# Expert 0's rows gathered before the last token tile is written, the last tile's rows added on TensorE, two weight steps put off, and 20 places of small matmuls moved

## The chip, the cores and the metric

One core of one Trainium2 chip runs the whole program. The metric is the device time of one execution in microseconds (us), the median of several. TensorE (PE) multiplies matrices into PSUM, VectorE (DVE) and ScalarE (ACT) read PSUM and do elementwise work, GpSimd (POOL) does elementwise work and issues the indirect DMAs, SyncE (SP) issues the plain DMAs. Each engine works through its own instructions in order.

## What is computed

```
def _attn_ref(q, k, v):                       # B, H, S, D = 4, 8, 768, 64
    for t in range(S):
        state = gamma * state + outer(k[:, :, t], v[:, :, t])
        y[:, :, t] = scale * q[:, :, t] @ state

def _moe_ref(x, w_in, w_out):                 # 3072 x 512, 512 x 2048, 2048 x 512
    h = x @ w_in
    sp = np.where(h > 20.0, h, np.log1p(np.exp(np.minimum(h, 20.0))))
    return (h * np.tanh(sp)) @ w_out

def _moe2_ref(x, w_gate, w1, w2):             # 8 experts of 384 tokens each
    logits = x @ w_gate
    # all (token, expert) pairs in falling order of logit; a token goes to the first
    # expert that still has room (cap = N // E = 384)
    for e in range(E):
        mask = assigned == e
        out[mask] = np.maximum(x[mask] @ w1[e], 0.0) @ w2[e]
```

## The kernel before

Attention and the first feed-forward layer run over 8 groups of 384 tokens (`NG`, `G`), each of three tiles of 128 (`CPG`, `C`). `h_phase(g)` computes the hidden layer of a group into one of two buffers `G` (GB[0], GB[1]), `logits(g)` the gate's logits from it, and `x_phase(g)` the layer's output: 48 matmuls of 512 columns per tile into a PSUM bank "px", which ACT and DVE split into two half-precision parts (`xr`, with the row's scale in its last two places) and SP writes to the table `x_rows` in DRAM (L622). Every product is made of such high and low parts, three matmuls for one (`mm3`, L525, the line of nearly all matmuls).

Then come the experts. Expert r takes its 384 rows out of `x_rows` by three indirect DMAs (L890, issued on POOL) with the list of its tokens, `IDX[r]`. They are turned so that the model dimension lies on the partitions (`xt`): for expert 0 by 24 transposes on TensorE (L902) and three copies (L903), for the others by a DMA transpose (L354). `expert(r)` runs 96 matmuls of 384 columns (first half, weights W1) and 72 of 512 (second half, weights W2), with its weights in WIN (even r) or WOUT (odd r).

Beside this run three side programs. `route_round(r)` finds by five digits (0, 2, 4, 6, 8 in the names below) which tokens round r gives to which expert: for each digit a comparison on DVE (L686), 24 small matmuls `pc`, a small DVE step (L731), one matmul `pn`, and DVE again (L736, L740); at its end two matmuls `pp`. `route_list(r)` makes `IDX[r]` from it (L686 into `amt`, then 24 matmuls `pl`, L819). `weights(i)` loads the expert's weights W1 (i = 0) or W2 (i = 1) by an indirect DMA of 2 MB (L862) into one half of RAW, sums their squares on ACT (L868), totals them with one matmul `pt`, and splits them into two parts in four pieces (ACT L228 and DVE L229).

The order on TensorE is written out by the program: a `Weave` runs a main generator (the large matmuls) and after each piece of it the side programs that are due; a side program yields (wait, cost) in the planner's microseconds, most of them from the table `KN`. `KN['rs'][r]` holds the offsets of the 12 waits of round r, `KN['fs'][r]` those of the weight steps. ACT is in program order too from the last group on; the order on DVE and POOL is chosen by a scheduler. In the tail, `x_phase(7)` (3 tiles) is followed by the one tile of group 5 that was put off (`late`), then by `tokens()`, which gathers, and by `expert(0)`:

```
    wv.run(x_phase(NG - 1))
    wv.run(x_phase(NG - 3, late, GB[0]))
    XD.append(1)
    wv.add(tokens())
```

Of the kernel before, what the change touches and what calls it, by code (L numbers as in the profile page):

```python
# [1213 lines left out]
```

## Time and profile before

| | |
|---|---|
| median of 3 runs | 1097.4 us (1096.71 to 1100.52) |
| profiled execution | 1102.12 us, of which the span from the first to the last instruction is 1100.2 us |
| granted clock of TensorE, mean | 0.947 of full speed |
| busy in the span | PE 965.7, DVE 766.8, ACT 664.3, POOL 404.3 us |

Busy time is the time in which an engine had an instruction at work; matmuls are pipelined, so neighbouring ones overlap. Idle time of an engine that nobody waits for costs nothing.

### The profile page before, as it was taken

The numbers are of one execution on the slowest core, as the hardware profiler recorded it, in microseconds if no ns is written. First come the engines' busy times: TensorE is split into PE (matmuls) and PEld (weight loads), VectorE is DVE, ScalarE is ACT, GpSimd is POOL, SyncE is SP. The second block draws the span as 40 slices with busy tenths as digits, with TensorE's granted clock in tenths as the row PEclk, the third lists the DMA queues.
The fourth block names the chain that finished last, engine by engine and source line by source line (L and its number), as shares of the span: only waits on it lengthen the run. The fifth ranks groups of instructions, "written<-read, shape, count | busy, mean of one in ns | idle before, by whom it ended". The sixth has DMA issues, their size and how long they took to land.

```text
span 1100.2 us, 19751 instructions
## 1 busy us (share of the span) xinstructions
PE 965.7 (88%) x7897; PEld 558.3 (51%) x7897; DVE 766.8 (70%) x1742; ACT 664.3 (60%) x1010; POOL 404.3 (37%) x289
## 2 busy tenths in 40 slices
...
PEclk9959988878999999999999999999699999999999
...
GB/s 316 173 156 42 106 192 38 39 91 167 27 53 86 41 49 87 39 64 62 49 87 83 45 39 1 10 117 114 159 177 164 179 148 153 233 84 263 140 29 29
DMA packets 108812, 113.65 MB, mean 103 GB/s; under 512 B 92464, under 2 KB 92592, under 8 KB 106672
## 3 DMA queue, kind: packets, MB, share of 16 engines
q1 hardware_dynamic: 102576, 66.24, 23.5%
...
## 4 chain that ended last, share of the span: by engine, by line
PE 46%; DVE 23%; issue 12%; ACT 5%; DMA 4%; POOL 4%; SPq 0%; another core or an unknown queue 0%; POOLq 0%; ACTq 0%; DVEq 0%
PE ph L525 18%; PE px L525 18%; DVE ld L686 2%; DVE WIN L229 2%; DVE WOUT L229 2%; DMA yh<-WOUT 1%; DVE RAW L571 1%; DVE ld L373 1%; PE py L434 1%; POOL out_dram L937 1%; DVE G L574 1%; DVE RAW L555 1%; DMA ld<-in_qkv_dram 1%; DVE G L920 1%; DMA G<-x_rows,GQ 1%
## 5 line engine op out<-in xcount | busy, mean ns | idle before, releaser
L525 PE MATMUL ph<-xt,WIN 128*128 128x384 f16 x1728 | 330.8, 334 | 14.2 <-DVE RAW L555 6.3
L525 PE MATMUL px<-WOUT,G 128*128 128x512 f16 x1248 | 312.9, 386 | 2.1 <-DVE WOUT L229 1.5
L525 PEld LDWEIGHTS <-WIN 128*128 128x128 f16 x1920 | 187.4, 101 | 155.6 <-issue 31.7
L525 PEld LDWEIGHTS <-G 128*128 128x128 f16 x1728 | 165.7, 99 | 185.9 <-issue 18.6
L577 POOL TENSOR_TENSOR G<-RAW,G 128x1536 f16<-128x1536 f32 (+1 forms) x32 | 102.0, 3186 | 98.1 <-DVE G L574 78.5
L555 DVE TENSOR_SCALAR RAW<-ph 128x384 f32<-128x384 f32 x124 | 68.2, 551 | 44.2 <-PE ph L525 43.7
L406 POOL TENSOR_TENSOR amt<-amt 128x512 f16<-128x512 f32 x40 | 53.6, 1341 | 122.7 <-DVE amt L403 85.9
L562 ACT ACTIVATE RAW<-RAW,zt,ch 128x1536 f32<-128x1536 f32 x32 | 53.3, 1666 | 43.8 <-DVE RAW L555 40.3
L325 ACT ACTIVATE junk<-ld 128x512 bf16<-128x512 f32 x63 | 39.6, 628 | 62.5 <-DMA ld<-in_qkv_dram 61.4
L868 ACT ACTIVATE junk<-RAW 128x1024 bf16<-128x1024 f32 x64 | 67.5, 1055 | 6.2 <-DMA RAW<-in_w1p_dram,MASK 5.5
L571 DVE TENSOR_TENSOR RAW<-RAW 128x1536 f32<-128x1536 f32 (+1 forms) x33 | 56.5, 1712 | 13.8 <-ACT RAW L570 13.7
L223 POOL TENSOR_TENSOR RAW<-ld,RAW 128x512 f16<-128x512 f32 x34 | 46.5, 1384 | 43.5 <-ACT RAW L222 41.8
L862 POOL DMA_INDIRECT RAW<-in_w1p_dram,MASK x8 | 8.0, 1000 | 144.0 <-ACT G L919 45.9
L228 ACT ACTIVATE WOUT<-RAW,se 128x1024 f16<-128x1024 f32 x32 | 36.0, 1148 | 35.3 <-DVE se L195 35.3
L920 DVE TENSOR_TENSOR G<-G,G 128x384 f16<-128x384 f32 x64 | 35.5, 554 | 31.3 <-ACT G L919 31.1
L400 DVE TENSOR_TENSOR amt<-pa,MASK 128x512 f32<-128x512 f32 x38 | 26.1, 687 | 37.7 <-PE pa L399 30.4
L525 PEld LDWEIGHTS <-WOUT 128*128 128x128 f16 x384 | 36.9, 99 | 24.1 <-issue 0.7
L937 POOL DMA_INDIRECT out_dram<-G,MASK x18 | 25.7, 1426 | 62.5 <-ACT G L936 57.3
L570 ACT ACTIVATE RAW<-RAW 128x1536 f32<-128x1536 f32 (+1 forms) x33 | 47.7, 1445 | 0.4
L563 ACT ACTIVATE RAW<-RAW 128x1536 f32<-128x1536 f32 x32 | 47.2, 1476 | 0.4
L525 PE MATMUL px<-WIN,G 128*128 128x512 f16 x192 | 45.3, 388 | 1.3 <-DVE G L920 0.8
L223 POOL TENSOR_TENSOR STH<-SC,STH 64x256 f16<-64x256 f32 x34 | 29.6, 871 | 45.1 <-ACT STH L222 42.2
...
## 6 DMA issues: line engine op xcount, KB each, us to landing
...
ld<-in_qkv_dram SPq DMA_DIRECT2D x3, 256.0 KB
```

What stands on the lines that cost most here:

```text
L223: (V if pool in ("V", "E") else P).tensor_tensor(lo, src, hi, op=OP.subtract)
L229: V.scalar_tensor_tensor(lo, src, s, hi, op0=OP.mult, op1=OP.subtract)
L406: (P if mode[1] == "P" else V).tensor_tensor(amh[:, j, 1], am, amh[:, j, 0], op=OP.subtract)
L525: T.matmul(p, a, b, start=i == 0, stop=i == n - 1)
L555: V.tensor_scalar(hs[:, f], p[:, :G], 1.0 / 65536.0, None, op0=OP.mult)
L562: A.activation(th, hs, AF.Tanh, scale=ch[:, q:q + 1], bias=z)
L563: A.activation(th, th, AF.Arctan, scale=-0.5, bias=0.5)
L570: A.activation(th[:, w], th[:, w], AF.Sin, scale=-2.0, bias=math.pi / 2)
L571: (V if hm[1] == 'V' else P).tensor_tensor(th[:, w], th[:, w], hs[:, w], op=OP.mult)
L577: (P if lo == 'P' else V).tensor_tensor(gb[:, 1, o], th[:, w], gb[:, 0, o], op=OP.subtract)
L868: A.activation(junk(1024), RAW[:, o:o + 1024], AF.Square, accum_out=ss[:, j:j + 1])
L920: V.tensor_tensor(hid[:, 1, f], hs, hid[:, 0, f], op=OP.subtract)
```

## The change

The tail is put into another order. First a tile of zeros is written over the last 128 rows of `x_rows`. Then come tiles 0 and 1 of group 7, the tile of group 5, and, as soon as the first list is there, the three gathers for expert 0 (`first_rows`), which find zeros in the place of the last tile's rows. The last tile of group 7 is computed after their issue. `first_x` then turns the gathered rows by multiplying them with the identity (24 matmuls of 128 columns, into PSUM as f32) and adds to each bank the last tile's rows straight from `xr` in SBUF, by 24 matmuls with a 0/1 matrix that says which of its rows belongs into which column (`FIRST["cols"]`, made on DVE in `route_list(0)`). Six copies, three on ACT and three on DVE, bring the sums to `xt`; before, 24 transposes and three copies on DVE did it. The rows are gathered a second time, after the last tile has been written, only for the scales in their last two places, into the buffers of expert 1's rows, from where three DVE copies in `prep_x(1)` save them.

Two weight steps are put off: the loads of expert 1's weights wait in the program until the first gathers are issued, and the four pieces of expert 0's W2 are split after `first_x`. In the table, 20 of the 96 entries of `rs` change (rounds 1 to 7; one of round 1, two of round 2, the rest of rounds 3 to 7) and one of `fs`; one round's line shows what such a change looks like.

```diff
-rs=[..., [1.46, -2.35, 0.04, -0.29, 0.13, -2.18, 0.42, -0.4, 0.45, 0.03, 1.16, -4.07], ...
+rs=[..., [-1.04, -2.35, 0.04, -0.29, 0.13, -0.18, -1.58, -0.4, 0.45, 0.03, 3.56, -5.57], ...
-fs=[..., [0.0, -1.5, -0.61, 0.29]]
+fs=[..., [0.0, -1.5, 2.89, 0.29]], ..., g0=[0.5, 2.2, 1.5]
@@ -620,9 +620,11 @@
                 V.tensor_scalar(xr[:, 2 * DM:].bitcast(F32), i_t, cx, None, op0=OP.mult)
             r = g * G + c * C
             SY.dma_start(xbuf[r:r + C, :], xr)
+            XR[0] = xr
             yield PC[0] * 0.216
 
 
+    XR, FIRST = [None], {}
     RT, IDX, EWI, EWF = {}, {}, {}, []
 
     def route_setup():
@@ -813,6 +815,14 @@
         V.tensor_scalar(pjv, pjf[:, 0, :, None].to_broadcast([128, NT, VR]), 1.0, None, op0=OP.add)
         for t in range(0, NT, 8):
             against(oh[:, t:t + 8], pjv, OP.is_equal, len(DIGITS) - 1, slice(t, t + 8))
+        if r == 0:
+
+            e3 = rt("e3", [CPG], BF)
+            for jt in range(CPG):
+                V.tensor_scalar(e3[:, jt:jt + 1], pjf[:, 1, NT - 1:], float(jt), None, op0=OP.is_equal)
+            FIRST["cols"] = rt("cols", [CPG, C], F16)
+            V.tensor_tensor(FIRST["cols"], oh[:, NT - 1, None, :].to_broadcast([128, CPG, C]),
+                            e3[:, :, None].to_broadcast([128, CPG, C]), op=OP.mult)
         yield max(0.0, KN['lw'] + KN['rs'][r][11]), 0.0
         pl = ps.tile([128, CPG, 2], F32, name=f"pl{r}x11x", tag="pm")
         for t in range(NT):
@@ -847,7 +857,7 @@
     def weights(i):
         src = (w1p, w2p)[i]
         for r in range(E):
-            while r not in EWI or (r == 1 and KN['ga'][i] and 0 not in XTE):
+            while r not in EWI or (r == 1 and ((KN['ga'][i] and 0 not in XTE) or "rows" not in FIRST)):
                 yield 0.5, 0.0
             W = EWB[r % 2]
             ei = EWI[r]
@@ -869,7 +879,8 @@
                 yield KN['qs'], 0.0
             yield max(0.0, KN['tw'] + KN['fs'][r][2 + i]), 0.2
             SW[i, r] = pow2(total(ss, 4, "tote", f"pt{r}x{2 + i}x"), f"se{i}", 3)
-            while (r > 1 and r - 2 not in (H2, OUT)[i]) or (r == 1 and not XD):
+
+            while (r > 1 and r - 2 not in (H2, OUT)[i]) or (r == 1 and not XD) or (r == 0 and i and 0 not in XTE):
                 yield 0.5, 0.0
             for j in range(4):
                 o = i * 4096 + j * 1024
@@ -882,26 +893,61 @@
                 V.tensor_scalar(ie, SW[0, r][1], SW[1, r][1], 65536.0, op0=OP.mult, op1=OP.mult)
                 SC[r] = ie
 
+    def first_rows():
+
+        for c in range(CPG):
+            P.indirect_dma_start(out=XG[c], out_offset=None, in_=xbuf,
+                                 in_offset=bass.IndirectOffsetOnAxis(ap=IDX[0][:, c:c + 1], axis=0))
+        FIRST["rows"] = True
+
+    def first_x():
+
+        xt = wk.tile([128, 2, KD, G], F16, name="xt", tag="xt", bufs=2)
+        XTE_[0] = xt
+        pp = {}
+
+        def part(c, a, w, cols, first):
+            if first:
+                pp[c, a] = ps_any().rearrange("p (k t) -> p k t", k=KD)
+            for k in range(KD):
+                o = (a * KD + k) * 128
+                T.matmul(pp[c, a][:, k], w[:, o:o + 128], cols, start=first and k == 0, stop=not first and k == KD - 1)
+            if not first:
+                o = xt[:, a, :, c * C:(c + 1) * C]
+                with tc.high_priority():
+                    if a:
+                        V.tensor_copy(o, pp[c, a])
+                    else:
+                        A.activation(o, pp[c, a], AF.Copy)
+
+        yield KN['g0'][0], 0.0
+        for c in range(2):
+            for a in range(2):
+                part(c, a, XG[c], identh, True)
+        yield KN['g0'][1], 1.0
+        for c in range(CPG):
+            for a in range(2):
+                if c == 2:
+                    part(c, a, XG[c], identh, True)
+                part(c, a, XR[0], FIRST["cols"][:, c, :], False)
+
+        for c in range(CPG):
+            P.indirect_dma_start(out=XG[CPG + c], out_offset=None, in_=xbuf,
+                                 in_offset=bass.IndirectOffsetOnAxis(ap=IDX[0][:, c:c + 1], axis=0))
+        yield KN['g0'][2], 1.7
+
     def prep_x(r):
         xt = wk.tile([128, 2, KD, G], F16, name="xt", tag="xt", bufs=2)
         XTE_[r] = xt
+        if r == 1:
+            FIRST["scale"] = rt("fs", [CPG])
+            for c in range(CPG):
+                V.tensor_copy(FIRST["scale"][:, c:c + 1], XG[CPG + c][:, 2 * DM:2 * DM + 2].bitcast(F32))
         for c in range(CPG):
             xg = XG[(r % 2) * CPG + c]
             P.indirect_dma_start(out=xg, out_offset=None, in_=xbuf,
                                  in_offset=bass.IndirectOffsetOnAxis(ap=IDX[r][:, c:c + 1], axis=0))
-            if r:
-                turned(xt, c, xg[:, :2 * DM])
-        if r == 0:
-
-            yield 10.0, 0.0
-            for c in range(CPG):
-                p = ps_any().bitcast(F16).rearrange("p (a k t) -> p a k t", a=2, k=KD)
-                for a in range(2):
-                    for k in range(KD):
-                        o = (a * KD + k) * 128
-                        T.transpose(p[:, a, k], XG[c][:, o:o + 128], identh)
-                V.tensor_copy(xt[:, :, :, c * C:(c + 1) * C], p)
-            return
+            turned(xt, c, xg[:, :2 * DM])
         yield KN['gx'], 0.0
 
     def expert(r):
@@ -921,10 +967,13 @@
             yield PC[0] * 0.163
         while r not in SC:
             yield 0.5
+        while r == 0 and "scale" not in FIRST:
+            yield 0.5
         fac = rt("fac", [CPG], bufs=3)
         for c in range(CPG):
             xg = XG[(r % 2) * CPG + c]
-            V.tensor_scalar(fac[:, c:c + 1], xg[:, 2 * DM:2 * DM + 2].bitcast(F32), SC[r], None, op0=OP.mult)
+            xs = xg[:, 2 * DM:2 * DM + 2].bitcast(F32) if r else FIRST["scale"][:, c:c + 1]
+            V.tensor_scalar(fac[:, c:c + 1], xs, SC[r], None, op0=OP.mult)
         H2.add(r)
         for c in range(CPG):
             p = ps_any()
@@ -1073,8 +1122,11 @@
         for r in range(E):
             while r not in IDX or (r > 0 and r - 1 not in RUN) or (r > 1 and r - 2 not in H2):
                 yield 1.0, 0.0
-            yield KN['tk'], 0.0
-            yield from prep_x(r)
+            if r:
+                yield KN['tk'], 0.0
+                yield from prep_x(r)
+            else:
+                yield from first_x()
             XTE[r] = XTE_[r]
 
     wv = Weave(tc)
@@ -1147,8 +1199,14 @@
     wv.run(x_phase(NG - 2))
     for c in late:
         SY.dma_start(GB[0][:, :, :, c * C:(c + 1) * C], gbuf[c])
-    wv.run(x_phase(NG - 1))
+    zr = wk.tile([128, ROW], F16, name="xr", tag="xr", bufs=2)
+    V.memset(zr, 0.0)
+    SY.dma_start(xbuf[N - C:, :], zr)
+    wv.run(x_phase(NG - 1, range(CPG - 1)))
     wv.run(x_phase(NG - 3, late, GB[0]))
+    need(lambda: 0 in IDX)
+    first_rows()
+    wv.run(x_phase(NG - 1, range(CPG - 1, CPG)))
     XD.append(1)
     wv.add(tokens())
     for r in range(E):
```

On POOL, from the first weight load of the experts on (`in_w1p_dram` and `in_w2p_dram` are W1 and W2, `x_rows` the gathers, `out_dram` the scatters of finished rows), before:

```order
172 L862 DMA RAW<-in_w1p_dram,MASK 128x4096
173 L862 DMA RAW<-in_w2p_dram,MASK 128x4096
174 L862 DMA RAW<-in_w1p_dram,MASK 128x4096
175 L890 DMA G_67<-x_rows,MASK 128x1026 x6
176 L862 DMA RAW<-in_w2p_dram,GQ 128x4096
177 L862 DMA RAW<-in_w1p_dram,MASK 128x4096
178 L937 DMA out_dram<-G_67,MASK 3072x512
```

and in the changed kernel:

```order
172 L872 DMA RAW<-in_w1p_dram,MASK 128x4096
173 L872 DMA RAW<-in_w2p_dram,MASK 128x4096
174 L872 DMA RAW<-in_w1p_dram,MASK 128x4096
175 L899 DMA G_67<-x_rows,MASK 128x1026 x3
176 L935 DMA G_67<-x_rows,MASK 128x1026 x3
177 L948 DMA G_67<-x_rows,MASK 128x1026 x3
178 L872 DMA RAW<-in_w2p_dram,GQ 128x4096
179 L872 DMA RAW<-in_w1p_dram,MASK 128x4096
```

The first gathers (L899) still stand behind expert 1's W1 load, the third load; between them and expert 1's gathers (L948) stand the second gathers for the scales (L935).

On TensorE, between the last large matmul of the last tile and expert 0's first (`identh` is the identity, `xt` expert 0's turned rows), before:

```order
11431 L729 MATMUL pc2x2x<-MASK,ld 128x8
11432 L734 LDWEIGHTS onesb
11433 L734 MATMUL pn2x3x<-MASK,onesb 128x8
11434 L185 MATMUL pt1x2x<-sse_8619,onesf 128x4
11435 L902 LDWEIGHTS G_67
11436 L902 MATMUL ph<-identh,G_67 128x128
...
11483 L525 LDWEIGHTS WIN
11484 L525 MATMUL px<-xt,WIN 128x384
```

and in the changed kernel (`STH` holds the 0/1 matrix):

```order
11285 L525 MATMUL px<-WOUT,G_68 128x512
11286 L914 LDWEIGHTS G_67
11287 L914 MATMUL ph<-identh,G_67 128x128
...
11318 L731 LDWEIGHTS ld
11319 L731 MATMUL pc2x0x<-MASK,ld 128x8
...
11366 L829 LDWEIGHTS amt
11367 L829 MATMUL pl1x11x<-GQ,amt 128x6
...
11414 L914 LDWEIGHTS xr
11415 L914 MATMUL ph<-STH,xr 128x128
```

Of round 2, before had `pc` and `pn` of digits 0 and 2 ahead of the transposes; now the first digit's `pc` and list 1's `pl` stand between the 16 identity matmuls of the first two row tiles and the matmuls with the 0/1 matrix, and `pc2x2x` comes only inside expert 0.

On DVE, from the end of round 1 to the last tile's eviction (`WIN` is expert 0's weights, `xr` the tile), before:

```order
1024 L779 COPY MASK<-pp1x10x 128x48
1025 L229 SCALAR_TENSOR_TENSOR xr<-px,st,xr 128x512
1026 L781 SCALAR_TENSOR_TENSOR MASK<-MASK 128x48
1027 L229 SCALAR_TENSOR_TENSOR WIN<-RAW,se_8544,WIN 128x1024
1028 L783 TENSOR_TENSOR GQ<-MASK 128x48
1029 L229 SCALAR_TENSOR_TENSOR WIN<-RAW,se_8544,WIN 128x1024
1030 L784 TENSOR_TENSOR GQ<-GQ,pp1x10x 128x48
1031 L229 SCALAR_TENSOR_TENSOR WIN<-RAW,se_8544,WIN 128x1024
```

and in the changed kernel, a little later in the same stretch:

```order
1061 L688 TENSOR_TENSOR ld<-MASK,ld 128x3072
1062 L192 TENSOR_SCALAR sta<-sst 128x1
1063 L688 TENSOR_TENSOR amt<-GQ,ld 128x1024
1064 L195 TENSOR_SCALAR st<-sta 128x1
1065 L196 TENSOR_SCALAR st<-sta 128x1
1066 L688 TENSOR_TENSOR amt<-GQ,ld 128x1024
1067 L620 TENSOR_SCALAR xr<-st,cx 128x1
1068 L229 SCALAR_TENSOR_TENSOR xr<-px,st,xr 128x512
1069 L688 TENSOR_TENSOR amt<-GQ,ld 128x1024
```

The four pieces of W2 (three of them shown) are gone from this stretch and stand inside expert 0; the last tile's `xr` now follows the comparison of round 2's first digit and two of list 1's three.

## Rows read from the trace of the kernel before

**Rows 1.** Page, head and part 2: 40 equal slices of 27.5 us, tenths of full clock.

```profile
span 1100.2 us, 19751 instructions
...
PEclk9959988878999999999999999999699999999999
```

**Rows 2.** Windows by stage: length, busy us of each engine, PEclk, DMA share, GB/s.

```profile
core 0: us, PE busy (x) PEld busy (x) DVE busy (x) ACT busy (x) POOL busy (x), PEclk, DMA share, GB/s
...
775.75:794.94 19.19, 5.82 (x102) 5.30 (x102) 15.29 (x58) 5.98 (x11) 7.57 (x6) 0.56 0.45 151
794.94:814.59 19.65, 18.76 (x164) 10.90 (x164) 13.19 (x35) 9.81 (x18) 0.94 (x1) 0.90 0.69 161
814.59:853.02 38.43, 36.26 (x320) 19.93 (x319) 33.06 (x102) 25.94 (x45) 11.16 (x8) 1.00 0.55 172
853.02:891.19 38.17, 35.33 (x317) 19.63 (x315) 32.28 (x97) 26.77 (x47) 11.33 (x8) 1.00 0.60 173
891.19:931.19 40.00, 36.17 (x311) 19.91 (x311) 31.51 (x100) 24.36 (x42) 8.46 (x8) 0.96 0.50 165
931.19:974.24 43.05, 38.18 (x324) 20.77 (x324) 33.63 (x109) 26.76 (x47) 10.88 (x8) 0.96 0.51 153
974.24:1092.17 117.93, 116.65 (x671) 61.52 (x669) 54.63 (x137) 69.25 (x121) 25.40 (x21) 1.00 0.39 123
```

**Rows 3.** Timeline of PE around expert 0's start: start, us, instructions, idle before.

```profile
770.41 5.34 PE L525 MATMUL px<-WOUT,G 128*128 128x512 f16 x24
...
782.77 0.80 PE L729 MATMUL pc2x0x<-MASK,ld 128*128 128x8 bf16 x24 [7.01 <-DVE ld L686]
...
784.07 0.95 PE L819 MATMUL pl1x11x<-GQ,amt 128*128 128x6 bf16 x24
...
791.07 1.01 PE L902 MATMUL ph<-identh,G 128*128 128x128 f16 x8
...
794.94 3.95 PE L525 MATMUL px<-xt,WIN 128*128 128x384 f16 x12 [1.14 <-DVE se0a L192]
...
801.48 2.12 PE L525 MATMUL px<-xt,WIN 128*128 128x384 f16 x12
```

**Rows 4.** The chain that ended last, in order of time, same stretch.

```profile
778.98 2.68 DMA x_rows<-xr
781.99 0.72 issue
782.71 4.38 DMA G<-x_rows,MASK
```

**Rows 5.** Timeline of DVE, same stretch.

```profile
771.68 1.28 DVE L229 SCALAR_TENSOR_TENSOR WIN<-RAW,se,WIN 128x1024 f16<-128x1024 f32 x1
...
778.20 0.75 DVE L229 SCALAR_TENSOR_TENSOR xr<-px,st,xr 128x512 f16<-128x512 f32 x1
...
782.61 1.30 DVE L686 TENSOR_TENSOR amt<-GQ,ld 128x1024 bf16<-128x1024 bf16 x2
...
783.89 0.70 DVE L686 TENSOR_TENSOR amt<-GQ,ld 128x1024 bf16<-128x1024 bf16 x1
```

**Rows 6.** Timelines of POOL, ACT and SP: a weight load, and gathers behind one.

```profile
770.78 0.94 POOL L862 DMA_INDIRECT RAW<-in_w1p_dram,MASK  x1 [32.28 <-ACT xr L228]
...
780.00 1.06 ACT L868 ACTIVATE junk<-RAW 128x1024 bf16<-128x1024 f32 x1 [1.83 <-DMA RAW<-in_w1p_dram,MASK]
...
912.62 0.96 POOL L890 DMA_INDIRECT G<-x_rows,MASK  x1 [0.30 <-issue]
...
920.83 4.02 SPq L354 DMA_TRANSPOSE xt<-G  x3
```

**Rows 7.** The chain, 985 to 1012 us: another gather behind a weight load.

```profile
991.08 2.16 POOL RAW L862
...
993.72 9.00 DMA G<-x_rows,GQ
```

**Rows 8.** Who PE waited for, 794 to 985 us: total, times, longest (first of 17).

```profile
PE pc6x8x L729 <- DVE ld L686: 2.4, 1, 2.4
```

**Rows 9.** Timeline of PE in expert 7: W2's total, and the second half's first matmuls.

```profile
1046.06 0.28 PE L185 MATMUL pt7x3x<-sse,onesf 128*128 128x4 f32 x2
...
1076.47 5.34 PE L525 MATMUL ph<-WOUT,G 128*128 128x512 f16 x24
```

More of the change, by code (lines that the diff above doesn't have):

```diff
@@ L37 @@
 UNIT = [256.0 ** i for i in reversed(range(len(DIGITS)))]
-KN = dict(ea=1, sc=1, pw=4, le=0.0, hl=['P', 'P'], cs=['V', 'V', 'V', 'V', 'V', 'V', 'V'], cc=['V', 'V', 'V', 'V', 'V', 'V', 'V', 'V', 'V'], lo=['c0', 'g', 'c1', 'm', 'c2', 's', 'wg', 'w0', 'w1', 'w2'], ga=['', 'V'], rs=[[-0.63, 0.3, -1.2, 0.0, 0.24, 0.0, 0.09, 0.0, 0.21, 0.0, 0.0, -4.24], [2.1, 0.09, 2.19, 0.0, 0.58, 0.15, 0.18, 0.15, 0.26, 0.26, 1.46, -0.41], [3.26, 0.0, -0.68, 0.2, 0.33, 0.0, -0.3, 0.0, 0.09, -0.12, 0.3, -3.18], [0.56, 0.0, 0.38, 0.0, 0.15, 0.0, 0.12, -0.11, -0.04, -0.27, 0.03, -3.34], [0.67, 0.0, 0.31, -0.76, 0.89, 0.0, 0.15, -0.22, 0.0, 0.0, -0.16, -4.15], [1.46, -2.35, 0.04, -0.29, 0.13, -2.18, 0.42, -0.4, 0.45, 0.03, 1.16, -4.07], [0.45, 0.54, 0.45, 0.0, 1.18, 0.0, -0.39, -0.55, -0.61, -0.05, 0.45, -3.57], [-0.15, 0.0, -0.75, 0.0, 0.0, 0.0, 0.0, -0.3, 0.0, 0.0, 3.28, -3.01]], fs=[[0.0, 0.0, -3.96, -1.22], [-0.75, 0.0, 1.32, 0.16], [0.0, 0.0, -2.08, 0.13], [0.0, -1.13, 0.71, 0.36], [0.0, 0.0, 0.0, -0.56], [0.38, 0.75, 0.13, 0.04], [0.0, 0.38, 0.2, 0.69], [0.0, -1.5, -0.61, 0.29]], av=[5.75, 5.75, 2.0, 4.0], a2=[1.3, 2.2, 4.3], a1=[0.1, 1.0, 0.85], ao=[3.5, 3.5, 3.35], wv=[8.5, 0.5, 1.0, 4.5], ov=5.0, an=[3.0, 3.15, 3.6], qm=['P0', 'VP', 'VP', 'PH', 'P1', 'VV', 'VP'], vm=['P0', 'VP', 'VP', 'VP', 'VP', 'P0', 'VP'], km=['A', 'H', 0, 0, 0, 0, 0], am=['AP', 'AP', 'AP', 'AV', 'AP', 'AV', 'VP'], ss=['V', 'P', 'P', 'P', 'P', 'P', 'P'], sm=['P', 'V', 'V', 'P', 'E', 'D', 'P'], ym=[0, 0, 0], hm=['VVVP', 'VVAV', 'VVVP', 'VVVP', 'AVVP', 'VVVP', 'VVVP', 'VVVP', 'VVVP'], ci=['AP'] * 8, co=['AP'] * 8, wa=[15, 12, 8, -1, 7, 16], cp=[0, 100, 0, 100], np=0, yp=[0, 2000], op=[0, 0, 200, 0, 50, 1000], xp=[0, 0, 0, 0, 0, 0], ld=[0, 1, 2, 3, 4], wj=[4, 4, 4], fw=[13.5, 18.5, 14, 16, 14, 16], qs=1.0, tw=3.0, sw=1.5, po=[[0] * 8] * 4, sl=[0, 0, 0.7], rw=[4.9, 2.5, 1.55, 1.7, 1.7], pn=0.5, lw=14.0, gx=9.0, tk=2.75, st=[16.0, 21.0, 20.0, 23.5], wi=['H', 'A', 0, 0, 2, 0, 0, 0], wo=['H', 'H', 0, 0, 0, 0, 'H', 0], tp=[], gw=5.15, nw=1.0, cw=0, sp=50, ap=1000, wp=None, ip=None)
```

1 line of the change is left out of this document (added).

## The prediction

> **What bounds the kernel now.** I read the page first, then windows cut at the seams of the tail, then the timelines of the worst window. The page's slices show one place where TensorE's clock falls to 0.6, the slice from 770 to 798 us [rows 1]. The windows say why [rows 2]: from 775.75 us, the end of the last `x_phase` matmul (770.41 + 5.34, [rows 3]), to 794.94, expert 0's first matmul, PE is busy for 5.8 of 19.2 us. After that three stages differ. Up to 974 us, while the routing runs, PE idles 0.9 + 2.2 + 2.8 + 3.8 + 4.9 = 14.6 us (length less busy) and DVE is busy 78 to 86% from round 3 on. After 974 us PE is busy for 116.7 of 117.9 us: there the end is TensorE work, so a microsecond won ahead of it reaches the end unless it is lost in the routing stretch.
>
> In the gap the chain is: the tile's eviction up to 778.95 [rows 5], its write to DRAM 2.68, 0.72 of waking POOL, then the first gather's 4.38 [rows 4]; meanwhile PE waits 7.0 us for DVE, which is late with round 2 [rows 3]. Expert 0's first 12 matmuls then take 3.95 us against 2.12 later [rows 3]: the clock is at its lower level (1.2 GHz), 0.56 in this window, and these 1.83 us belong to the gap's price.
>
> **The change, part by part,** in the clock times of the profile of before. The work of the four tiles ahead of 775.75 is the same, only its order differs.
>
> *Gathers.* They no longer wait for the last tile. They wait for group 5's tile, now third, written about where before's third tile was, and they stand on POOL behind expert 1's W1 load (770.78 + 0.94, [rows 6]). So the first starts near 772.5. How long it takes has two bounds. With nothing ahead it took 4.38 [rows 4], which gives 776.9. Behind a weight load it took 9.00 [rows 7] and 920.83 - 912.62 = 8.2 (up to the transposes that use it, [rows 6]). Here a 2 MB load stands 1 us ahead and lands at 780.0, 9.2 after its issue [rows 6], so I take the nearer rows, 9.0: landing at 781.5, the other two by about 782.8 (one POOL issue each, behind it). The Trainium skill, "DMA: Bandwidth & Descriptors", section "SWDGE vs HWDGE vs iDMA", says that only one queue is allocated for GpSimd's DMAs and that an engine drains a ring packet by packet, which speaks against this change's early issue: by it the gather lands behind the load, and by a free queue it would land some 4.6 us earlier; both figures are those of the rows just named, and the two rows behind a load agree with the page.
>
> *DVE.* Three pieces of W2's split, 1.28 each, go from the stretch between round 1's end and round 2's comparison: 3.84 us. Before, list 1's third comparison ended at 783.89 + 0.70 = 784.6 [rows 5]; now it ends near 780.75. The tile's `xr` (0.75) stands just ahead of it and is ready near 780.1, 1.1 later than before: that the eviction is later costs nothing, since list 1's matmuls stand ahead of its use and need the third comparison. The new 0/1 matrix and its helpers on DVE lie beside `x_phase` matmuls, under 1 us of a stretch with a tile still to go; without that cover they would cost about that 1 us.
>
> *TensorE.* From 781.5: 16 identity matmuls at 1.01 for 8 [rows 3], 2.0 us, to 783.5; `pc2x0` 0.80 and list 1's 0.95, to 785.25; 16 with the 0/1 matrix, 2.0, to 787.3; the third row tile's 8 + 8, 2.0, to 789.3; a copy, about 0.75 like the other pass of DVE over 512 columns of PSUM [rows 5], to 790.0. The copies of the first two row tiles lie beside these matmuls. So expert 0 starts near 790.0, 4.9 us earlier. Before, the clock was back within 12 matmuls of expert 0, about 8 us after PE resumed at 791 with the transposes; now PE resumes at 781.5, about 8.5 us ahead of the expert, so I count the 1.83 as won too: **6.7 us**. Bounds: with a free gather DVE's 780.75 binds, the identity matmuls and `pc2x0` being done by then: 0.95 + 2.0 + 2.0 + 0.75 give 786.5, so 8.4 + 1.8 = 10.2. With the gather 3.6 later than taken (it also shares the drain with the other two, and POOL's own issue can take 2.16, [rows 7]) and a slow clock at the expert's start, 1.3.
>
> *Weights.* Expert 1's W1 load keeps its place on POOL. W2's four pieces (5.1 us on DVE) now fall into expert 0's first half. They are needed only at its second half, 96 matmuls or 17 us later; what they cost is DVE time in a stretch where it is busy 13.2 of 19.7 us [rows 2]. W2's load for expert 1 goes behind the second gathers and expert 1's gathers. Taking the write (2.7), POOL (0.7) and gather (4.4) after the `xr` at 780.1, the scales land from 788 on, and the load goes out near 794, as before; the scale copies ahead of W2's pieces on DVE wait a microsecond at most.
>
> *The moved matmuls.* I counted the order. Between round 2's `pp` and round 6's, before has 360 matmuls of 384 columns and 288 of 512; the changed kernel has 384 and 308. At 2.12/12 and 5.34/24 [rows 3] that is 24 x 0.177 + 20 x 0.2225 = 8.7 us more large work over the same four rounds. Ahead of round 2's `pp` expert 0 holds 8 and 24 more, 6.8 us, which about pays for the 5.1 us of W2 and the digit comparison (1.8) that are now done there. If DVE sets the rounds' pace, the 8.7 us fill waits like that of `pc6x8x` [rows 8], out of the 13.7 us that PE idles in these rounds. If the waits are short misfits in place, nothing is filled. I take **4 us**, below the middle, since DVE is not full; ends 8.7 and -5.1 (W2's pieces come back whole as waits).
>
> Sum: 6.7 + 4 = 10.7, less 0.7 for places where a moved matmul now meets a late operand: **10 us**. The profiled execution took 1102.1 (span 1100.2 and 1.9 around it), 4.7 above the median of 1097.4. Taken from the median, 10 us give 1087.4.
>
> **Rivals.** *The queue decides.* The gather comes only as the weight load lets it and the clock is still low: 1.3 at the start, 3 later, so 1093. For it speaks that both gathers behind a load were slow [rows 6, 7]; against it, that half of its delay is in my sum. This is the page's queue rule at its worst.
>
> *DVE decides.* The start is won but W2's 5.1 us return as waits in rounds 2 to 4, where DVE is fullest (33.1 of 38.4 us, [rows 2]): 6.7 - 5.1 = 1.6, so 1095.8. Against it: the matmuls were placed later by about as much.
>
> *Both ends pay out:* a free gather and all 8.7 us: 19, so 1078.5. It needs a gather that overtakes the load, which no row shows.
>
> *Slower: W2 arrives late for experts 5 to 7.* Before, expert 7's `pt7x3x` runs 1076.47 - 1046.06 = 30.4 us ahead of the second half [rows 9]; now 44 matmuls of 384 columns, 7.8 us, stand between. W2's load waits for the split of its predecessor, and ACT's sums of squares stand ahead of evictions, so a load landing late by d stops PE by d less the few us of slack in PSUM and lead, once per expert 5, 6 and 7. Beyond d = 5 us per expert it would cost more than the 10 won plus the 5.5 that count as slower: from there 1103 or more. Against it: a load takes 9.2 us [rows 6] and the second half alone over 15.
>
> **How the numbers follow.** Forecast 0.60 (own range 1082.5 to 1091.5), queue 0.14, DVE 0.13, both ends 0.07, W2 late 0.06. A change under 0.5% (5.5 us) can't be told from none here, so faster means under 1091.9 and slower over 1102.9. Faster holds the forecast, both ends and half of the queue case: 0.74; the other half and DVE's case are the same: 0.20; slower 0.06. The range 1081 to 1096 leaves out both ends, W2 late, and a little beyond DVE's case.
>
> **What would show it.** Right: expert 0's first matmul some 14 us after the last `x_phase` matmul, not 19; PE's wait in that gap ended by the gather; the first 12 matmuls near 2.1 us; less idle in rounds 4 to 6; no wait after round 7. Wrong: the gather landing within 5 us; PE waits for W2's pieces or for a `pt` in experts 5 to 7; DVE waiting long for the second gathers.

## The result

The changed kernel took 1087.76 us (median of 5 runs, 1085.86 to 1089.53), where the kernel before took 1097.4: ratio 0.9911, 95% interval 0.9887 to 0.9935. Forecast were 1087.4 and 1081 to 1096. On a second chip, where the kernel before took 1104.88, the changed one took 1091.46: 0.9888 (0.9873 to 0.9903). Its profiled execution took 1086.88, 0.9 below its median; that of [rows 1] took 1102.12, and a second trace of before 1104.55. So the traces lie 15 us apart and the medians 9.6 and 13.4. Before itself differs by 7 us between chips; every ratio below is against runs of before on the experiment's own chip.

The page, head and clock row, answers to [rows 1]: the slice at 0.6 is gone.

```profile
span 1085.0 us, 19820 instructions
...
PEclk9859889878999999999999999999999999999999
```

Windows by stage, cut as in [rows 2] at expert 0's first matmul, at the `pp` of rounds 2 to 6 and at the last matmul:

```profile
777.57:787.70 10.13, 5.96 (x97) 5.80 (x98) 6.77 (x18) 4.36 (x9) 1.22 (x2) 0.75 0.47 193
787.70:814.58 26.88, 25.08 (x226) 14.34 (x224) 24.27 (x58) 17.89 (x30) 6.79 (x6) 0.97 0.61 167
814.58:852.26 37.68, 36.48 (x324) 20.51 (x323) 33.15 (x100) 25.17 (x43) 13.65 (x8) 1.00 0.59 175
852.26:892.05 39.79, 38.80 (x336) 21.56 (x335) 33.37 (x100) 27.64 (x47) 13.17 (x10) 1.00 0.62 166
892.05:928.31 36.26, 34.02 (x312) 19.27 (x311) 31.20 (x97) 22.92 (x40) 7.47 (x7) 1.00 0.63 182
928.31:970.96 42.65, 40.48 (x344) 22.43 (x343) 35.05 (x109) 25.85 (x44) 14.07 (x10) 1.00 0.60 165
970.96:1076.64 105.68, 102.77 (x595) 53.83 (x593) 51.99 (x130) 68.34 (x118) 20.11 (x19) 1.00 0.42 133
```

The gap ahead of expert 0 is 10.1 us, not 19.2. In rounds 3 to 6 PE idles 1.20 + 0.99 + 2.24 + 2.17 = 6.6 us, not 13.7, at full clock throughout. The last stretch is 12.3 us shorter, since 595 matmul records are left where 671 were.

TensorE's timeline through the gap, POOL's, the chain and DVE's (against [rows 3 to 6]):

```profile
772.23 5.34 PE L525 MATMUL px<-WOUT,G 128*128 128x512 f16 x24
781.71 0.40 PE L914 MATMUL ph<-identh,G 128*128 128x128 f16 x4 [4.15 <-DMA G<-x_rows,MASK]
...
782.94 0.83 PE L731 MATMUL pc2x0x<-MASK,ld 128*128 128x8 bf16 x24
783.62 0.78 PE L829 MATMUL pl1x11x<-GQ,amt 128*128 128x6 bf16 x24
784.26 0.59 PE L914 MATMUL ph<-STH,xr 128*128 128x128 f16 x4
...
787.70 0.48 PE L525 MATMUL ph<-xt,WIN 128*128 128x384 f16 x1
788.62 2.36 PE L525 MATMUL ph<-xt,WIN 128*128 128x384 f16 x11 [0.44 <-DVE xt L919]
```

```profile
772.21 0.94 POOL L872 DMA_INDIRECT RAW<-in_w1p_dram,MASK  x1 [31.90 <-DVE MASK L772]
774.26 1.04 POOL L899 DMA_INDIRECT G<-x_rows,MASK  x1 [1.10 <-issue]
```

```profile
770.09 3.11 DMA x_rows<-xr
...
774.26 7.41 DMA G<-x_rows,MASK
```

```profile
781.13 0.75 DVE L229 SCALAR_TENSOR_TENSOR xr<-px,st,xr 128x512 f16<-128x512 f32 x1
781.80 0.68 DVE L688 TENSOR_TENSOR amt<-GQ,ld 128x1024 bf16<-128x1024 bf16 x1
```

PE's wait is ended by the gather, no longer by DVE; the gather took 7.4 us behind the weight load.

Where the gain sits is plainest in three windows for the two kernels traced on one chip: I from the end of the last `x_phase` matmul (the seam) to round 2's `pp`, II to round 6's `pp`, III to the last matmul. First before, then the changed kernel:

```profile
777.84:816.45 38.61, 24.42 (x264) 16.16 (x265) 28.44 (x91) 15.78 (x29) 8.58 (x7) 0.73 0.61 156
816.45:976.72 160.27, 145.54 (x1270) 80.17 (x1269) 130.48 (x403) 103.23 (x174) 40.92 (x32) 0.98 0.55 165
976.72:1094.70 117.98, 116.70 (x671) 61.50 (x669) 54.75 (x139) 69.61 (x123) 25.31 (x21) 1.00 0.39 123
```

```profile
776.10:813.39 37.29, 31.04 (x319) 20.17 (x320) 31.21 (x76) 22.29 (x38) 8.25 (x8) 0.91 0.55 174
813.39:974.25 160.86, 151.88 (x1314) 84.12 (x1313) 132.38 (x405) 101.69 (x173) 49.60 (x34) 0.99 0.56 167
974.25:1079.25 105.00, 102.72 (x595) 53.91 (x593) 52.08 (x130) 68.38 (x118) 20.15 (x19) 1.00 0.42 134
```

I and II together take 198.9 and 198.2 us: on this chip the routing did not get shorter. It got fuller: 6.6 and 6.3 us more PE work was done in it, and III is 13.0 shorter. The three differences, -1.3, +0.6 and -13.0, make 13.7, and the medians on that chip differ by 13.4. The first two traces divide the gain another way: there I and II went from 198.5 to 193.4 us and III became 12.3 shorter. II of the one changed kernel takes 156.4 us in its first trace and 160.9 in its second, so differences of II below some 4.5 us decide nothing, and how much of the gain is a shorter routing and how much a fuller one is not settled.

### The profile page after: what moved, and what is told of

It reads as the page before. It is cut to its first block, busy times and chain, and to the rows that moved or that the text cites. A ratio compares the mean times of both kernels' runs of the same rounds, so it can differ in the third digit from the quotient of the medians.

```text
span 1085.0 us, 19820 instructions
## 1 busy us (share of the span) xinstructions
PE 961.6 (89%) x7921; PEld 557.6 (51%) x7921; DVE 768.9 (71%) x1751; ACT 663.2 (61%) x1013; POOL 407.4 (38%) x292
## 4 chain that ended last, share of the span: by engine, by line
PE 47%; DVE 23%; issue 8%; ACT 7%; DMA 6%; POOL 3%; SPq 0%; POOLq 0%; ACTq 0%; DVEq 0%
PE ph L525 19%; PE px L525 19%; DVE WIN L229 2%; DVE WOUT L229 2%; DMA yh<-WOUT 1%; ACT junk L878 1%; DVE ld L373 1%; PE py L434 1%; DVE ld L688 1%; DVE G L966 1%; DVE RAW L571 1%; DVE RAW L555 1%; DMA RAW<-in_w1p_dram,MASK 1%; DMA ld<-in_qkv_dram 1%; DVE G L574 1%
## 5 line engine op out<-in xcount | busy, mean ns | idle before, releaser
L525 PE MATMUL px<-WOUT,G 128*128 128x512 f16 x1344 | 335.5, 386 | 2.9 <-DVE WOUT L229 1.5
L525 PEld LDWEIGHTS <-G 128*128 128x128 f16 x1728 | 165.1, 99 | 185.3 <-issue 14.8
L562 ACT ACTIVATE RAW<-RAW,zt,ch 128x1536 f32<-128x1536 f32 x32 | 53.3, 1664 | 42.4 <-DVE RAW L555 38.8
L616 ACT ACTIVATE junk<-px 128x512 bf16<-128x512 f32 x24 | 14.0, 584 | 57.2 <-PE px L525 57.2
L525 PE MATMUL ph<-WIN,G 128*128 128x512 f16 x192 | 44.8, 379 | 1.6 <-DVE G L966 0.8
L688 DVE TENSOR_TENSOR ld<-MASK,ld 128x1536 bf16<-128x1536 bf16 (+1 forms) x35 | 44.5, 1273 | 0.5
```

Of the source, the lines that this page charges most:

```text
L525: T.matmul(p, a, b, start=i == 0, stop=i == n - 1)
L562: A.activation(th, hs, AF.Tanh, scale=ch[:, q:q + 1], bias=z)
L688: V.tensor_tensor(out.rearrange("p t (j v) -> p t j v", v=VR), cv[:, ts, None, :].to_broadcast([128, n, J // VR, VR]), RT["jr"][:, i, :J]. ...
```

## The experiments

Two theories. A: the routing, a chain of small steps in which DVE answers each count, sets how long I and II take, and the change packs large matmuls into them. B: PE's work sets it, and the change wins the gap alone. The three windows of each kernel, with its ratio:

| kernel | ratio (interval) | I | II | III |
|---|---|---|---|---|
| changed, first trace | 0.9911 (0.9887 to 0.9935) | 37.0 | 156.4 | 105.7 |
| changed, again | 0.9888 (0.9873 to 0.9903) | 37.3 | 160.9 | 105.0 |
| before, first trace | 1 | 38.8 | 159.7 | 117.9 |
| before, again | 1 | 38.6 | 160.3 | 118.0 |
| front alone | 1.0032 (1.0019 to 1.0045) | 36.4 | 157.6 | 119.8 |
| moves alone | 1.0049 (1.0031 to 1.0066) | 38.0 | 163.2 | 114.6 |
| moves undone, squares kept | 1.0069 (1.0045 to 1.0093) | 38.5 | 164.8 | 120.1 |
| more DVE | 0.9939 (0.9918 to 0.9961) | 38.4 | 164.0 | 106.3 |
| W2 at once | 1.0206 (1.0169 to 1.0243) | 48.4 | 177.2 | 103.4 |
| W2 at once, gather ahead | 1.0081 (1.0051 to 1.0110) | 40.0 | 187.6 | 103.4 |
| gather ahead | 1.0000 (0.9976 to 1.0023) | 37.6 | 163.7 | 110.8 |
| gather ahead, scales on POOL | 0.9909 (0.9883 to 0.9935) | 39.9 | 165.1 | 106.2 |
| the same, front first | 0.9897 (0.9873 to 0.9920) | 38.9 | 163.6 | 108.9 |
| front first | 0.9912 (0.9896 to 0.9928) | 39.6 | 161.4 | 105.0 |

The windows are those of one traced execution each. Three of these lie well above the median of their kernel: 4.7 us ("W2 at once, gather ahead"), 6.9 ("scales on POOL") and 4.9 ("the same, front first"). They show which waits there are, not where the median's time goes.

**The front alone.** Tables `rs` and `fs` as before; rounds 1 and 4 shown, and `fs[7]`.

```diff
-[2.1, 0.09, 2.19, 0.0, 0.58, 0.15, 0.18, 0.15, 0.26, 0.26, 1.46, -4.41]
+[2.1, 0.09, 2.19, 0.0, 0.58, 0.15, 0.18, 0.15, 0.26, 0.26, 1.46, -0.41]
...
-[0.67, 0.0, 0.31, 0.24, 0.89, 0.0, 0.15, -0.22, 0.0, 0.0, 2.24, -7.15]
+[0.67, 0.0, 0.31, -0.76, 0.89, 0.0, 0.15, -0.22, 0.0, 0.0, -0.16, -4.15]
...
-[0.0, -1.5, 2.89, 0.29]
+[0.0, -1.5, -0.61, 0.29]
```

> The changed kernel with the 20 table entries for small matmuls (and the later place of expert 7's sum of squares) put back as they were; the early gathers, the 0/1 matmuls and the two put-off weight steps stay. Theory A (DVE sets the pace of the routing rounds, so the moved matmuls only fill waits of PE): between round 2's pp and round 6's the order holds 380 matmuls of 384 columns and 264 of 512 where the changed kernel has 384 and 308, 10.5 us less large work in the same rounds; PE's idle time there goes from 8 us to 12 or more, and the time is 1091 to 1095. Theory B (the whole gain is the gap ahead of expert 0, the moved matmuls are worth nothing): 1086 to 1089, like the changed kernel.

1101.35 us against 1097.84: not faster but 0.3% slower than before, beyond both expectations (and less than the 0.5% that the prediction takes for the least that can be told). Expert 0 starts 9.8 us after the seam, as in the changed kernel. Windows of rounds 3 to 6 and of III:

```profile
812.40:852.38 39.98, 37.34 (x320) 20.14 (x319) 33.64 (x106) 25.30 (x43) 13.90 (x8) 0.96 0.56 165
852.38:889.68 37.30, 34.48 (x317) 19.72 (x316) 31.71 (x95) 25.29 (x43) 10.21 (x8) 1.00 0.57 177
889.68:930.48 40.80, 36.29 (x315) 20.44 (x315) 32.66 (x102) 25.41 (x43) 7.95 (x8) 0.96 0.54 162
930.48:969.95 39.47, 34.85 (x315) 19.63 (x315) 32.62 (x101) 24.65 (x41) 13.17 (x8) 1.00 0.56 168
969.95:1089.70 119.75, 114.30 (x642) 59.88 (x641) 53.05 (x143) 70.48 (x121) 24.39 (x21) 0.97 0.42 121
```

The four rounds take 157.6 us, as long as in the changed kernel, with 10.5 us less large work in them; PE idles 2.64 + 2.82 + 4.51 + 4.62 = 14.6 us, and the work comes behind them. That is theory A. Where the median loses 3.5 us against before is not settled: there is no trace of before from this chip, and next to before's two traces this one is not longer from the seam on but 2.7 and 3.2 us shorter (313.7 against 316.4 and 316.9). I and II keep some 5 us of what the gap won (193.9 against 198.5 and 198.9); III is 1.8 us longer although it holds 5.0 us less large work (28 matmuls of 384 columns). Most of that loss is one long wait (timeline of PE, then the chain, which shows expert 7's W1 load taking 15.4 us, issued 2.1 us behind expert 6's W2 load):

```profile
889.68 0.18 PE L778 MATMUL pp4x10x<-MASK,tri 128*128 128x48 bf16 x1 [2.33 <-DVE MASK L753]
889.70 0.18 PE L779 MATMUL pp4x10x<-MASK,onesb 128*128 128x48 bf16 x1
889.73 4.12 PE L525 MATMUL ph<-WIN,G 128*128 128x512 f16 x12
...
1029.72 0.59 PE L185 MATMUL pt7x2x<-sse,onesf 128*128 128x4 f32 x2 [5.43 <-ACT junk L878]
```

```profile
1005.50 15.43 DMA RAW<-in_w1p_dram,MASK
```

**The moves alone.** The kernel before with the new `rs` and `fs`.

> The kernel before with the moved matmuls alone (its gap ahead of expert 0 stays 19 us, W2's split is not put off). Order: 392 matmuls of 384 columns and 288 of 512 between round 2's pp and round 6's, against 360 and 288 before, 5.7 us more large work. Theory A: 2 to 6 us faster than before, 1091 to 1095. Theory B: as before, 1096 to 1099. Third possibility: the moves fit only the new front, small matmuls stand where nothing needs them and routing slows down: slower than before.

1102.77 us, 0.5% slower: theory A's 1091 to 1095 fails, B's "as before" too, and the third possibility came. The trace bears it out in part only. II holds 5.7 us more large work and is 2.9 to 3.5 us longer than in the two traces of before, so some of its waits were filled (PE idles 10.6 us in it, not 13.7 or 14.7); the gap's second wait grew from 4.5 to 5.6 us (PE at `pc2x2x`), and groups of large matmuls ran at the lower clock at three places. From the seam on, the trace is 315.7 us long, no longer than before's 316.4 and 316.9. So the moves fill waits without the new front too, by 2 to 3 us, but the median gains nothing by it; what takes it back was not found.

**The moves undone, squares kept.** As the front alone, but `fs[7][2]` stays 2.89.

> The changed kernel with the 19 table entries for the rounds' small matmuls put back, but expert 7's sum of squares left at its later place (the run with that put back too took 1101.35 and showed one wait of 5.43 us for that sum, and 14.6 us of idle PE in rounds 3 to 6 against 6.6). Theory: that wait goes with its clock loss, and the rounds' idle stays: 1093 to 1097. Rival (the wait is ACT's lateness with expert 7's weights, not the place of the matmul, and comes back one matmul later): 1099 to 1102.

The edit puts back all 20 entries of `rs`, not 19. 1110.2 us against 1102.48. The wait at `pt7x2x` is gone, but 2.85 us came at `pt6x3x` and three of 0.8 to 1.0 behind it, II took 164.8 us, and the clock fell at five places. The rival is the nearer; why II is 7 us longer than with the front alone stays open. Undoing the moves costs 1.2 to 1.8% of the time whichever way the squares stand.

**More work on DVE.** The second piece of each split is done twice for experts 2 to 5.

```diff
+                if 2 <= r <= 5 and j == 1:
+                    V.scalar_tensor_tensor(W[:, 1, o:o + 1024], RAW[:, o:o + 1024], SW[i, r][0], W[:, 0, o:o + 1024],
+                                           op0=OP.mult, op1=OP.subtract)
```

> The changed kernel with one DVE pass of W1's and of W2's split done twice for experts 2 to 5 (the second writes the same values): 8 passes of 1.28 us, 10.2 us more DVE work between round 2 and round 6, nothing else moved. Theory A (DVE sets the pace of the rounds): rounds 3 to 6 grow by most of it, 5 to 10 us, and a clock loss or two comes on top; 1093 to 1100. Theory B (PE's work sets it and DVE, busy 83 to 88 percent, has room): 1087 to 1090.

0.9939, that is 0.28 or 0.51% above the changed kernel's two ratios, 3 to 6 us, between the theories; its interval overlaps that of the first of the two. II with its DVE time (columns as in the windows above):

```profile
816.42:980.44 164.02, 151.86 (x1313) 84.26 (x1312) 140.59 (x412) 101.86 (x173) 49.70 (x34) 0.99 0.53 163
```

DVE has 8.2 us more to do than in the changed kernel's second trace, II is 3.2 us longer than there, and PE idles 12.2 us in it, not 9.0. Against the first trace (156.4 us, DVE 132.8) it is 7.8 us more DVE and 7.6 more length. So DVE is the pace at least in part: between 40% of what it is given and nearly all comes out as length, and the two traces can't size it better.

**W2 at once.** Expert 0's W2 split is not put off.

```diff
-            while (r > 1 and r - 2 not in (H2, OUT)[i]) or (r == 1 and not XD) or (r == 0 and i and 0 not in XTE):
+            while (r > 1 and r - 2 not in (H2, OUT)[i]) or (r == 1 and not XD):
```

> The changed kernel, with expert 0's W2 split again as soon as it can be, ahead of expert 0's columns, instead of put off. If these 5.1 us of DVE matter where they stood (they held list 1's third comparison and the xr back), expert 0 starts 2 to 4 us later than in the changed kernel (3.84 us of DVE, of which the gather's lateness hides part) and the time is 1089 to 1092. If the gather alone decides when expert 0 starts, nothing changes: 1086.5 to 1088.5. If W2's pieces cost more in expert 0's first half than ahead of it, it is faster: 1083 to 1086.

1118.92 us, ratio 1.0206: some 20 us slower than before, far outside every expectation. The DMA queues (packets, MB, share of 16 engines) and issues (KB, us to landing) between 772 and 784 us, and PE:

```profile
q0 software_dynamic: 144, 2.10, 48.2%
q1 hardware_dynamic: 144, 0.26, 5.7%
...
x_rows<-xr SPq DMA_DIRECT2D x1, 256.5 KB, 8.7
RAW<-in_w1p_dram,MASK POOLq DMA_INDIRECT x1, 9.2
```

```profile
788.32 0.61 PE L914 MATMUL ph<-identh,G 128*128 128x128 f16 x4 [10.81 <-DMA G<-x_rows,MASK]
```

The four pieces delay the third tile's eviction, so its write is issued at 773.26, 0.7 us behind expert 1's W1 load instead of 2.1 ahead of it. It then lands after 8.7 us instead of 3.1, though SP issued it and POOL the load. The gather must wait for it, and PE idles 10.8 us. The kernel before holds the same collision unseen: there the third of the four last tiles is written at 771.50, 0.72 us behind the load, and that write lands after 8.6 us, but nothing waits for it.

**W2 at once, the gather ahead.** The same, with the W1 load made to wait for the gathered rows; `fs[1][0]` goes from -0.75 to 7.25, so that the sum of its squares stands later.

```diff
+            if r == 1 and i == 0:
+                ei = rt("ei0", [1], I32)
+                P.tensor_scalar(ei, XG[CPG - 1][:, 0:1], 0.0, EWF[0], op0=OP.mult, op1=OP.add)
```

> Expert 0's W2 split at once (1118.92, where the third tile's write left 0.7 us after expert 1's W1 load and took 8.7 us to land against 3.1) together with that load issued only after the first gathers. Collision theory: the write takes about 3 us again, the first gather starts near 778.5 instead of 783, PE's wait for it shrinks from 10.8 us to under 4, and the time falls by 6 us or more: 1100 to 1112. Rival (the 5.1 us of DVE work themselves did it): the wait stays over 8 us, 1115 or more.

1112.46 us against 1102.48, just above the collision theory's 1112. PE's waits for the gather are 3.24 + 0.93 us (forecast: under 4), I falls from 48.4 to 40.0, and the ratio from 1.0206 to 1.0081: the collision is shown. What is left sits in II: 17.3 us at `pc4x8x` (8.2 without the load moved), behind W2 pieces of expert 3 on DVE, whose load took 26.4 us to land behind two writes of output rows. In the same stretch the DMA transposes of gathered rows took 23.8 us (median) instead of 5.1. Why both took so long was not settled.

**The gather ahead.** The same two edits in the changed kernel.

> The changed kernel, with expert 1's W1 load issued only after expert 0's first gathers have landed (one small POOL instruction on the gathered rows ahead of it); its squares stand 8 us later on ACT. Queue theory: the first gather takes 4.4 us instead of 7.4, and expert 0 starts 2 to 3 us earlier after the last x_phase matmul (7.5 to 9 us instead of 10.1); time 1084 to 1086.5. Rival: the gather is slow for another reason (writes to DRAM, three gathers at once) and still takes 7 us or more: 1087 to 1089. Second rival: the later weights of expert 1 hold up its second column of matmuls: 1090 or more.

1098.76 us: the queue theory's mechanism came, its gain did not; the time is in the second rival's range. The gathers' median to landing is 3.6 us and expert 0 starts 9.3 us after the seam (PE, and DVE's wait behind it):

```profile
777.95 0.40 PE L917 MATMUL ph<-identh,G 128*128 128x128 f16 x4 [0.85 <-DMA G<-x_rows,MASK]
780.99 0.39 PE L917 MATMUL px<-identh,G 128*128 128x128 f16 x4 [2.64 <-DVE xr L229]
...
792.89 0.76 PE L731 MATMUL pc2x2x<-MASK,ld 128*128 128x8 bf16 x24 [2.62 <-DVE GQ L948]
```

Now the second gathers stand behind the load, DVE waits 2.9 us at the copy of their scales, and PE behind DVE. II is 163.7 us, and III holds 6.45 us of waits (2.9 in the changed kernel), 4.28 of them in one place.

**The scales on POOL.**

```diff
-                V.tensor_copy(FIRST["scale"][:, c:c + 1], XG[CPG + c][:, 2 * DM:2 * DM + 2].bitcast(F32))
+                P.tensor_copy(FIRST["scale"][:, c:c + 1], XG[CPG + c][:, 2 * DM:2 * DM + 2].bitcast(F32))
```

> The kernel whose W1 load waits for the first gathers (1098.76; expert 0 started 9.3 us after the last x_phase matmul, but DVE then stood 2.9 us at the copy of the scales, since the second gathers were behind the load, and PE 2.6 us behind DVE), with the three scale copies on POOL instead of DVE. If that stall was what ate the gain: no wait of PE at pc2x2, 1091 to 1096. If the later weights of expert 1 and their followers ate it: 1097 to 1100.

1093.67 us, as forecast for the stall, and no wait at `pc2x2`; but a wait of 3.04 us stands one step later, at `pn2x3x`, in a trace of 1100.60 us, the slowest of the six runs. By the medians the stall took most of the gain; the trace alone would not show that. The chain shows the collision a second time: the last tile's write, 1.05 us behind the load (782.81), took 8.4 us.

```profile
783.86 8.43 DMA x_rows<-xr
```

**The front first.** `pc2x0` and list 1 behind the gathering matmuls: `g0` from [0.5, 2.2, 1.5] to [0.5, 0.0, 2.7], and with the load and the scales moved too to [0.5, 0.0, 3.2].

> The changed kernel with round 2's pc2x0 and list 1's matmuls (0.83 + 0.78 us in its trace) placed behind the matmuls that gather expert 0's columns instead of between them; the order is otherwise the same. Expert 0's first matmul then starts 1 to 1.6 us earlier and round 2's first answer comes about 1.5 us later. Theory A (the routing chain on DVE sets the pace up to round 6): the round ends as late or later, and the time is that of the changed kernel, 0 to 2 us more. Theory B (PE's work sets it): 1 to 1.6 us less.

1094.7 us, 3.2 above the changed kernel on that chip, as A has it or a little worse. Nothing was won at the start either: `pc2x0x`, list 1 and round 2's `pn2x1x` still stand ahead of expert 0, `pn2x1x` waits for DVE, and expert 0 starts 11.2 us after the seam.

> W1's load behind the first gathers and the scale copies on POOL (0.9909 of before on another chip), with pc2x0 and list 1's matmuls placed behind the gathering matmuls as well. In the trace without this last step PE waited 2.97 us for the eviction of the last tile before the last of its identity matmuls, so that wait, not the small matmuls, decides when expert 0 starts: 0.989 to 0.992, no better than the changed kernel. If the small matmuls decide it, 1.5 us better: 0.986 to 0.989.

1092.7 us. Expert 0 starts 8.6 us after the seam, the earliest of all, behind a wait of 2.80 for the `xr` eviction. But its first 12 matmuls then take 4.00 us, at the lower clock, where the changed kernel's take 2.84; the time is that of the changed kernel within the intervals. No version beats it.

**Both kernels again.**

> The changed kernel itself once more, to stand beside the others on one chip. The first measurement gave 0.9911 of before. If that holds from chip to chip: 0.989 to 0.993; if part of it belonged to that chip: 0.993 to 1.0.

> The kernel before, for a second trace: the profiled execution shown lay 4.7 us above the median of the runs. If that excess is clock lost behind waits in rounds 4 to 6 (two places of about 1.5 us there), this trace has fewer of them; if it lies in the gap ahead of expert 0, the gap is shorter than 19.2 us here; if it lies ahead of the routing rounds, both are as before.

0.9888, so the gain holds. The second trace of before has the same gap (19.13 us), 14.7 us of idle in II where the first has 13.7, and the same two rounds (5 and 6) at the lower clock, and its run of 1104.55 is near the median of its chip, 1104.88; so the 4.7 us by which the profiled execution lay above the median look like a difference between chips, not like a place in the program.

## Why the prediction was right, and which terms were off

The mechanism was right: the gap closed by the early gathers, and the moved matmuls filled waits. The time was right to 0.4 us on the first chip, and that closeness is luck: the gain is 9.6 us there and 13.4 on the second chip, and between the traces, from which the terms were read, the sum of 10 should have been 15. By step:

*Gathers.* Start 3.3 us ahead of the seam, as forecast (772.5 against 775.75; 774.26 against 777.57), but by luck. The forecast let the first gather start as soon as POOL was free behind the load, and left out the landing of the third tile's write, which in before is issued at 771.50 and takes 8.6 us. In the changed kernel, with W2's pieces gone from DVE, that write is issued 7.5 us ahead of the seam instead of 4.3, in front of the load, and lands after 3.1. "W2 at once", where it is issued 4.3 us ahead again, shows what the term left out could have cost. Taken were 9.0 us behind the load, measured 7.4 (7.4 to 8.0 in six traces of five kernels with the load ahead, 3.6 without it). The choice of the rows behind a load was right. The Trainium skill, "DMA: Bandwidth & Descriptors", section "SWDGE vs HWDGE vs iDMA", with its one queue drained packet by packet, fits these gathers. The same page's "Queues, rings and completion order" has an engine take turns between queues, packet by packet, and SP's small writes fit that too: in "W2 at once" the profile counts 144 packets on each of the two queues, 0.26 MB for the write and 2.10 for the load, so taking turns ends them together, and they landed after 8.7 and 9.2 us, near 782.0 and 781.7.

*DVE.* Third comparison forecast 5.0 us after the seam, measured 4.9; `xr` ready 4.35, measured 4.3. That the tile's eviction costs nothing held.

*TensorE in the gap.* This term was mis-sized: 8.5 us from the gather to expert 0, measured 6.0 (781.71 to 787.70). The identity matmuls and `pc2x0` were priced from rows at the lower clock: the 16 ahead of `pc2x0` took 1.2 us instead of 2.0, and of the copy 0.44 showed. With the earlier landing the start came 9.1 us earlier, not 4.9. Of the clock's 1.83 about 1.1 came: expert 0's first 12 matmuls take 0.48 + 2.36 = 2.84 us, not 2.1.

*Weights.* W2's load went out at 800.5, 22.9 us behind the seam and not 18.3 (794), and no wait shows it; the scale copies waited 0.3.

*Moved matmuls.* The second mis-sized term: 4 us taken, and idle in rounds 3 to 6 fell by 7.1 (5.8 in the second pair of traces), near the upper bound of 8.7; two places of about 1.5 us at the lower clock in rounds 5 and 6, which no term held, went in the first trace and one of them in the second. The 0.7 for misfits was 0.9 in expert 0's first stretch and 1.6 in III, where PE waits three times in experts 5 and 6:

```profile
1000.98 0.39 PE L525 MATMUL px<-WOUT,G 128*128 128x512 f16 x1 [0.80 <-DVE G L966]
...
1032.48 1.30 PE L525 MATMUL ph<-WIN,G 128*128 128x512 f16 x4 [0.71 <-DVE WIN L229]
1034.62 0.39 PE L525 MATMUL ph<-WIN,G 128*128 128x512 f16 x1 [0.84 <-DVE G L966]
```

"No wait after round 7" was thus wrong by 2.4 us. Only the 0.71 is a wait for weights (W2 of expert 6), the rival of late weights in small; the other two are for the last piece of the hidden layer, and before has one such wait of 0.81. With the front alone late weights cost 5.4 us at `pt7x2x`, so that rival is real.

The traces' sum: gap idle 13.37 - 4.17 = 9.2, rounds 7.1, less 0.9 and 1.6, and 3.6 of PE's busy time (the clock, net of the added matmuls), 17.4 of 316.4 - 299.1 = 17.3 us from the seam on. The seam itself came 1.8 us later (777.57 against 775.75), 1.7 earlier in the second pair.

*The form of the sum* failed. It adds a front of 6.7 and moves of 4; measured alone, the front is 3.5 us slower than before and the moves 4.9 slower, and only together do they gain 10 to 13. One reading is that a gap closed ahead of a timeline of fixed length pays only by the work that is then placed inside it. It fits the second pair of traces, but it is not shown: with the front alone I and II are some 5 us shorter than before's, and late weights in III take that back, while with the moves alone waits of II are filled. Why neither part gains by itself stays open. The rivals "queue" and "DVE decides" each hold a part: the gather did wait for the load, and I and II did not shrink in the second pair of traces, and by 5.1 us in the first.
